# Loading the first two input tiles of a fused attention and gated-linear kernel as half tiles on two DMA queues

## The chip, the cores and the metric

The kernel runs on one core of one Trainium2 chip. The metric is the device time of one execution in microseconds. Each job runs the kernel before and the kernels under test in turn on one chip; different jobs may have different chips. All runs told of here were of the undisturbed (fast) state by the usual test (within 1.5% of the fastest of the same kernel).

Engines: PE does matmuls, PEld loads its weights, DVE, ACT and POOL do element work, SP and ACT issue DMAs. All times inside an execution are counted from the start of its span.

## The reference, cut to what matters

```python
x = A_x                                        # 2048 x 512, bf16
xn = _layernorm(x, axis=-1)
return x + _A_ref(xn, A_wqkv, A_w_phi, A_wo) + _B_ref(xn, B_w_gate, B_w_up, B_w_down)
# _A_ref: linear attention, 32 heads of 16, softmax feature maps; v = xn @ wqkv[:, 1024:1536]
# _B_ref: ((xn @ w_gate) * (xn @ w_up)) @ w_down, inner width 1792
```

Everything needs `xn`, so nothing useful can start before the first rows of `x` have landed, been centred and been transposed.

## The kernel before

The 2048 rows are 16 tiles of 128 rows. For the first four tiles the kernel splits the mean: ACT sums the second 256 columns and DVE the first 256; DVE then centres, PE transposes, ACT or DVE copies the transposed halves out of PSUM, and PE starts on the value projection (`v_matmul`). The scaling by the standard deviation is applied later. The `warm` calls are dummy matmuls.

```python
    sc.pin = True                       # pinned: each engine keeps this order
    load_x(0, 1)                        # tile 0, 128 KB, SP's queue
    load_x(1, 1, ACT)                   # tile 1, 128 KB, ACT's queue
    load_x(2, 1)
    load_v(ACT, 1)                      # value weights, quarters 1, 0, 3, 2
    load_v(SP, 0)
    load_v(ACT, 3)
    load_v(SP, 2)
    load_x(3, 1)
    load_gu(SP, 0, (1,))                # first slice of w_up
    act(sbf("lnv", 0, 1), eps_f, ["eps"], ["pace"])
    load_gu(ACT, 0, (0,))               # first slice of w_gate
    load_gu(SP, 1)
    ...
    def ln_mean_split(t):
        act(xn_tile(t)[:, 256:], x_tile(t)[:, 256:], [("x", t)], [("mu", t)], scale=1.0 / 512.0,
            accum=mu[:, t:t + 1])
        dve(lambda e: e.tensor_scalar(out=xn_tile(t)[:, :256], in0=x_tile(t)[:, :256], scalar1=1.0 / 512.0,
                                      scalar2=0.0, op0=ALU.mult, op1=ALU.add, accum_out=mua[:, t:t + 1]),
            [("x", t)], [("mua", t)], 256)
    ...
    warm(7)                             # 7 dummy matmuls of 512 columns
    warm(1, 512, [("x", 0)])            # one more when tile 0 is there
    sc.pin = True
    ln_mean_split(0)
    ln_mean_split(1)
    ln_center_split(0)                  # DVE; needs both sums
    ln_center_split(1)
    x_transpose(0, 2, 0)                # tile 0, first half; copied out by ACT
    ln_mean_split(2)
    x_transpose(0, 3, 1)
    warm(1, 128)
    x_transpose(1, 4, 0, DVE)           # tile 1, first half; copied out by DVE
    ln_center_whole(2)
    x_transpose(1, 5, 1, DVE)
    warm(1, 128)
    for t in range(2):
        v_matmul(t, t, ((1,), (0,)), stop=False)
    x_transpose(2, 6, 0)
    ...
```

The softmax here doesn't subtract the row's maximum and nothing guards it: scores larger than these inputs give would overflow.

## Time and profile before

| | before |
|---|---|
| time, first job | 214.42 us (214.38 to 214.47, 3 runs) |
| span of the traced execution | 212.6 us |
| PE busy | 98% of the span |
| tiles 0 and 1 landed | 3.68 and 3.84 us |
| first transpose on PE | 4.78 us |
| first gate matmul | 8.98 us |

The page says at once what the limit is. First come the span, PE's line of busy times, and the chain that ended last, by engine:

```profile
span 212.6 us, 4047 instructions
...
PE 208.8 (98%) x1476; PEld 125.6 (59%) x1476; DVE 165.8 (78%) x281; ACT 144.6 (68%) x350; POOL 108.8 (51%) x137
...
PE 97%; DMA 1%; DVE 1%; issue 0%
```

The chain in order of time (start, duration, what) shows, at its start, the only stretch but the last half microsecond (DVE, at 210.0 us) in which that chain is not PE's:

```profile
0.79 2.89 DMA arena<-in_A_x_dram
...
3.70 0.57 DVE arena L427 x3
...
4.46 0.27 DVE arena L434
...
4.78 0.65 PE ps L474 x4
```

Tile 0 lands at 0.79 + 2.89 = 3.68 us, DVE sums tiles 0 and 1 (L427) and centres (L434), PE transposes (L474). The timeline of PE (start, duration, engine, line, operation, shapes, count) goes on from there; the lines of dummy matmuls are left out:

```profile
4.78 0.65 PE L474 MATMUL ps<-arena 128*128 128x128 bf16 x4 [0.39 <-DVE arena L434]
...
5.33 0.63 PE L474 MATMUL ps<-arena 128*128 128x128 bf16 x4
...
5.87 1.33 PE L247 MATMUL ps<-arena 128*128 128x512 bf16 x4
...
7.25 2.33 PE L247 MATMUL ps<-arena 128*128 128x512 bf16 x12
```

The view puts twelve matmuls from 7.25 us on one line. The first eight, of 512 columns, start every 0.216 us; the last four, of 256 columns and from 8.98 us, are the first gate matmuls. The four from 5.87 us are the first value matmuls; they start at 5.87, 6.29, 6.60 and 6.82, so the first ran at half rate (0.427 us for 512 columns) and the full rate was there at about 6.5 us.

### The profile page before, as it was taken

To read this page: it belongs to the slowest core of one execution; us is meant where nothing else is said; L and a number is where in the kernel's file an instruction comes from. 1 tells how busy PE (TensorE), PEld (TensorE's weight loads), DVE (VectorE), ACT (ScalarE), POOL (GpSimd) and SP (SyncE) were. 2 spreads that over 40 slices of the span, in tenths; PEclk is the share of its full clock that TensorE was granted. 3 is DMA by queue.
4 is the path that set the end of the run, shared out by engine and by line. 5 is a ranking of instruction groups with operands and counts; after the bars stand their busy time and mean duration, and the time that the engine had idled before them with its cause. 6 is when DMAs were issued, how large, how long until landed. Compare 5 with 4: busy or idle time off the path is not lost.

```text
span 212.6 us, 4047 instructions
## 1 busy us (share of the span) xinstructions
PE 208.8 (98%) x1476; PEld 125.6 (59%) x1476; DVE 165.8 (78%) x281; ACT 144.6 (68%) x350; POOL 108.8 (51%) x137
## 2 busy tenths in 40 slices
PE   7999999999999999999999999999999999999995
PEld 2665444444554444444444444456888898899884
DVE  3686699998986647758989989896888898897622
ACT  4459998885989999987878977564544444432220
POOL 4030393243312448998895472204658549558540
DMA  5999119479500320331321223414265836556511
GB/s 166 305 283 372 65 35 187 89 200 328 104 3 0 49 49 3 60 59 33 72 53 26 49 52 49 104 54 65 48 80 131 190 70 135 125 128 148 123 49 49
DMA packets 49252, 22.29 MB, mean 105 GB/s; under 512 B 38097, under 2 KB 47697, under 8 KB 49233
## 3 DMA queue, kind: packets, MB, share of 16 engines
q1 hardware_dynamic: 48272, 21.39, 43.4%
q10 hardware_dynamic: 960, 0.66, 1.0%
q8 instruction: 11, 0.18, 0.4%
q14 instruction: 9, 0.07, 0.1%
HBM read 11.03 MB, written 2.10 MB: 62 GB/s over the span
## 4 chain that ended last, share of the span: by engine, by line
PE 97%; DMA 1%; DVE 1%; issue 0%
PE ps L247 91%; PE ps L553 2%; PE ps L611 2%; DMA arena<-in_A_x_dram 1%; PE ps L381 1%; PE ps L474 1%; DVE arena L427 0%; DVE arena L924 0%; DVE arena L434 0%; PE ps L1001 0%
## 5 line engine op out<-in xcount | busy, mean ns | idle before, releaser
L247 PE MATMUL ps<-arena 128*128 128x512 bf16 (+2 forms) x1160 | 200.0, 330 | 0.0
L247 PEld LDWEIGHTS ps<-arena 128*128 128x128 bf16 (+1 forms) x1160 | 110.9, 98 | 73.4 <-ACT arena L228 0.3
L228 ACT ACTIVATE arena<-ps 128x512 bf16<-128x512 f32 (+3 forms) x117 | 59.3, 538 | 17.9 <-PE ps L247 12.4
L228 ACT ACTIVATE arena<-arena 128x32 f32<-128x32 f32 (+8 forms) x131 | 52.4, 424 | 6.0 <-DVE arena L894 3.0
L894 DVE TENSOR_TENSOR arena<-ps,arena 128x512 f16<-128x512 f32 (+1 forms) x56 | 38.3, 685 | 19.5 <-ACT arena L228 14.2
L516 POOL TENSOR_TENSOR arena<-arena 128x1024 bf16<-128x1024 bf16 x16 | 31.0, 1934 | 38.0 <-ACT arena L228 38.0
L228 ACT ACTIVATE arena<-ps,arena 128x512 bf16<-128x512 f32 (+1 forms) x55 | 35.5, 671 | 10.1 <-PE ps L247 10.0
L506 DVE TENSOR_REDUCE arena<-arena 128x64 f32<-128x1024 bf16 x32 | 38.6, 1210 | 3.3 <-ACT arena L228 3.3
L855 POOL TENSOR_TENSOR arena<-arena 128x256 f16<-128x256 f16 x32 | 24.3, 768 | 13.0 <-DMA arena<-arena 11.7
L228 ACT ACTIVATE ps<-ps 128x256 f32<-128x256 f32 x24 | 8.8, 368 | 29.0 <-PE ps L247 29.0
L833 DVE TENSOR_TENSOR arena<-arena 128x896 f16<-128x896 f16 x32 | 23.7, 749 | 3.2 <-PE ps L247 3.1
L924 DVE SCALAR_TENSOR_TENSOR arena<-ps,arena 128x256 bf16<-128x256 f32 (+1 forms) x24 | 13.5, 569 | 10.4 <-PE ps L247 10.0
L773 POOL TENSOR_TENSOR arena<-arena 128x512 f16<-128x512 bf16 x14 | 16.2, 1175 | 4.7 <-DVE arena L894 3.3
L959 POOL TENSOR_TENSOR arena<-arena 128x512 f32<-128x512 f32 x8 | 9.5, 1192 | 17.1 <-ACT arena L228 17.1
L522 POOL TENSOR_TENSOR arena<-arena 128x512 bf16<-128x512 bf16 x16 | 17.2, 1074 | 0.9
L621 DVE TENSOR_TENSOR arena<-ps,arena 128x512 f16<-128x512 f32 x16 | 11.0, 687 | 1.4
L405 DVE BATCH_NORM_STATS2 arena<-arena 128x6 f32<-128x512 bf16 x16 | 10.4, 672 | 0.4 <-DMA arena<-in_A_x_dram 0.4
L520 POOL TENSOR_TENSOR arena<-arena 128x32 f32<-128x32 f32 x16 | 4.2, 266 | 9.5 <-ACT arena L228 9.5
L668 DVE BATCH_NORM_STATS2 arena<-arena 128x6 f32<-128x512 bf16 x14 | 9.0, 681 | 0.0
L553 PEld LDWEIGHTS ps<-arena 128*128 128x128 bf16 x128 | 6.0, 97 | 3.5
L802 DVE TENSOR_TENSOR arena<-arena 128x1792 f16<-128x1792 f16 (+1 forms) x8 | 7.0, 903 | 0.0
L611 PEld LDWEIGHTS ps<-arena 128*128 128x128 bf16 x128 | 6.2, 97 | 1.2
(54 smaller groups left out, 68.1 us busy)
## 6 DMA issues: line engine op xcount, KB each, us to landing
arena<-in_A_x_dram SPq DMA_DIRECT2D x8, 256.0 KB, 3.3
out_dram<-arena SPq DMA_DIRECT2D x15, 128.0 KB, 2.0
arena<-in_B_w_down_dram SPq DMA_DIRECT2D x1, 1792.0 KB, 7.9
arena<-in_A_x_dram SPq DMA_DIRECT2D x3, 512.0 KB, 4.2
arena<-arena SPq DMA_TRANSPOSE x44, 3.0
arena<-in_B_w_gate_dram SPq DMA_DIRECT2D x1, 640.0 KB, 8.7
arena<-in_B_w_up_dram SPq DMA_DIRECT2D x1, 640.0 KB, 9.9
arena<-in_B_w_gate_dram SPq DMA_DIRECT2D x1, 512.0 KB, 5.3
```

The costliest lines, as they stand in the source:

```text
L228: return sc.step(ACT, lambda e: e.activation(out=out_ap, in_=in_ap, func=func, scale=scale, **kw), reads, writes, 130.0 + 0.833 * n)
L247: ins = e.matmul(out_ap, lhsT=l, rhs=r, start=start and i == 0, stop=stop and i == npair - 1, **kw)
L506: dve(lambda e: e.tensor_reduce(out=sm, in_=e_v, axis=AX.X, op=ALU.add), [(name, s, 0), (name, s, 1)], [("sums", sr)], 1024)
L516: pool(lambda e: e.tensor_tensor(out=e_w, in0=e_w, in1=r_w, op=ALU.mult), [(name, s, 0), (name, s, 1), ("rs", n)], [(name, s, 0), (name, s ...
L522: pool(lambda e: e.tensor_tensor(out=e_v[:, :, 1, :], in0=e_v[:, :, 1, :], in1=rat[:, :, None].to_broadcast([128, H, 16]), op=ALU.mult), [ ...
L611: ins = e.matmul(bank(b0 + c // 4, (c % 4) * CW, CW), lhsT=ph[:, c, :], rhs=kvz_v[:, c, :], start=True, stop=True)
L621: dve(lambda e: e.tensor_tensor(out=o_tile(t).rearrange("p (b h f) -> p b h f", b=2, f=16), in0=nd[:, :, :, 0:16], in1=w_v[:, r].unsqueeze ...
L773: pool(lambda e, ft=ft: e.tensor_tensor(out=hH_v[:, ft, 0:512], in0=hT_v[:, ft, 0:512], in1=r2w, op=ALU.mult), [("hT", ft, 0), "r2w", ("x" ...
L833: dve(lambda e, k=k, i0=i0, i1=i1, op=op: e.tensor_tensor(out=s_block(p, k), in0=i0, in1=i1, op=op), ks + more, [s_key(p, k)] + over.get(k ...
L855: pool(lambda e, k=k, i0=i0, i1=i1, op=op: e.tensor_tensor(out=so_block(p, k), in0=i0, in1=i1, op=op), ks + [("so", p, m) for m in more], ...
L894: dve(lambda e: e.tensor_tensor(out=h_v[:, ft, sg * 512:(sg + 1) * 512], in0=bank(bu), in1=g, op=ALU.mult), [("ps", bu), ("g", s)] + ([("j ...
L924: dve(lambda e: e.scalar_tensor_tensor(out=o, in0=src, scalar=inv, in1=resid, op0=ALU.mult, op1=ALU.add), keys + [rkey, "inv"], [("ostg", ...
```

## The change

The intent is to begin sooner: the two halves of a tile go out on two queues at once, and each engine waits only for the half that it sums. The first slice of `w_gate` moves to SP's queue, both tiles use value weight quarter 1 before quarter 0, and a small constant that DVE made while idle is made later.

```diff
+    def load_x_half(t, h, eng):
+        c = slice(h * 256, h * 256 + 256)
+        o, i = x_tile(t)[:, c], rows(x_flat, t, 1)[:, 0, c]
+        sc.dma(eng, lambda e: e.dma_start(o, i), [], [("x", t) if h else ("x", t, 0)], 65536)
 ...
-    load_x(0, 1)
-    load_x(1, 1, ACT)
+    for t in range(2):
+        load_x_half(t, 0, SP)
+        load_x_half(t, 1, ACT)
 ...
+    act(sbf("lnv", 0, 1), eps_f, ["eps"], ["pace"])
+    load_gu(SP, 0, (0,))
     load_gu(SP, 0, (1,))
-    act(sbf("lnv", 0, 1), eps_f, ["eps"], ["pace"])
-    load_gu(ACT, 0, (0,))
 ... (in ln_mean_split, DVE's part)
-            [("x", t)], [("mua", t)], 256)
+            [("x", t, 0) if t < 2 else ("x", t)], [("mua", t)], 256)
 ...
-    for t in range(2):
-        v_matmul(t, t, ((1,), (0,)), stop=False)
+    for q in (1, 0):
+        for t in range(2):
+            v_matmul(t, t, ((q,),), start=q == 1, stop=False)
 ... (the constant epsz: made after the fourth tile's value matmuls, not at the start)
```

More of the change, by code (lines that the diff above doesn't have):

```diff
@@ L361, in _build, with eps_z @@
     pool(select(m4, ALU.is_ge, 0.0, 0, [[-32, 4], [0, HC]], 1), ["const"], ["mask"], CW)
-    dve(lambda e: e.tensor_reduce(out=epsz, in_=m1, axis=AX.XY, op=ALU.add), ["mask16"], ["epsz1"], 64)
-    dve(lambda e: e.tensor_scalar(out=epsz, in0=epsz, scalar1=1e-6, scalar2=None, op0=ALU.mult), ["epsz1"], ["epsz"], 1)
+    def eps_z():
+        dve(lambda e: e.tensor_reduce(out=epsz, in_=m1, axis=AX.XY, op=ALU.add), ["mask16"], ["epsz1"], 64)
+        dve(lambda e: e.tensor_scalar(out=epsz, in0=epsz, scalar1=1e-6, scalar2=None, op0=ALU.mult), ["epsz1"],
+            ["epsz"], 1)
     pool(select(m4, ALU.is_ge, 0.0, 31, [[32, 4], [0, HC]], -1), ["mask"], ["mask"], CW)
@@ L1042, in _build @@
     u1a()
+    eps_z()
     sc.pin = False
```

## The prediction

> **What bounds the kernel now.** The page gives a span of 212.6 us with PE busy 98%; the chain that ended last is PE 97%, DMA 1%, DVE 1%. By the chain in order of time, tile 0's load runs 0.79 to 3.68 us, then DVE sums (0.57 us) and centres (0.27 us), and the first transposes start at 4.78 us. In the PE timeline, from about 6.8 us the 512-column matmuls follow each other every 0.216 us without gaps. So the change can win only in the first 6.8 us, if no load that it delays is then waited for.
>
> **What changes.** By the order of instructions, PE, DVE, ACT and POOL compute as much as before; SP issues two more DMAs, ACT's queue one more half tile and no gate slice. The constant moves from an idle DVE (2.85 to 3.26 us) to about 14 us, costing DVE some 0.2 us off the critical path. PE's order changes only in that both tiles use weight quarter 1 before quarter 0.
>
> **Gain.** Before, tiles 0 and 1 (128 KB each, one per queue) shared the DMA engines and landed at 3.68 and 3.84 us. Now the first 128 KB is all of tile 0. In the packet records a 1024-byte packet takes 46 ns and a 512-byte one (first gate slice) 27 ns: the same bytes cost 17% more, but half a tile is ready sooner. [...] So only order is won. Estimates: tile 0's halves land at 3.3 (SP) and 3.5 us (ACT's first packets come 0.4 us later), tile 1's at 3.8 to 4.0. The in-order DVE sums tile 1 before it centres tile 0, so the first centring waits for tile 1's first half: about 3.8 + 0.34 = 4.12 us against 4.38. First transpose about 4.5 us: 0.25 us earlier.
>
> **What eats it.** PE runs at half rate (0.427 us per 512 columns) until about 6.5 us. [...] if the change of rate stays near 6.5 us, PE enters its dense stretch only 0.13 to 0.2 us earlier. The value weights are issued 0.4 us later but are bandwidth-limited: quarter 1 at 5.04 to about 5.3 us, needed at 5.6; quarter 0 about 5.9, needed at 6.3. First gate slice: 7.4 to about 7.8 us, needed at 8.8. Later loads slip by 0.8 us, with over 2 us of slack on PE.
>
> **Predicted** 214.2 us (before 214.42), 0.1% faster; range 213.9 to 214.55. Faster by over 2%: 0.005; within 2%: 0.99; slower by over 2%: 0.005.
>
> **What would show it.** First DVE sum at 3.3 to 3.4 us, not 3.70; first transpose 4.4 to 4.6, not 4.78; first full-rate matmul still near 6.5; dense stretch and all later pieces of the chain 0.1 to 0.25 us earlier; no PE wait for a weight load.
>
> **What would make it wrong.** Four half loads with as many packets as four whole ones may land no sooner (first DVE sum above 3.6 us, or tile 1's half above 4.1): no gain or a small loss. A late value weight or gate slice would show as a PE wait for a DMA at 5.6 to 9 us. Tiles 4 to 7 landing late could block the in-order DVE near 16 us.

Two passages are cut above, where marked. The forecast's sum is 214.42 us less about 0.2 us at the start of the dense stretch, 214.2 us.

## The result, and the profile after

213.93 us median (213.83 to 214.20, 6 runs) against 214.44 us (213.79 to 214.71, 6 runs) for the kernel before. The ratio is 0.9981 with a 95% interval of 0.9966 to 0.9995. (A ratio here is the mean time of one kernel's fast-state runs over that of the other's in the same rounds, so it is not quite the ratio of the two medians.) So the time falls by 0.2%: clear of zero.

The page after, first its span and PE's busy time, then the chain by engine:

```profile
span 212.2 us, 4050 instructions
...
PE 208.5 (98%) x1476; PEld 125.2 (59%) x1476; DVE 166.0 (78%) x281; ACT 144.7 (68%) x350; POOL 108.7 (51%) x137
...
PE 97%; DMA 1%; DVE 1%; SPq 0%; issue 0%
```

The chain in order of time, after:

```profile
0.79 0.39 SPq L277
...
1.24 2.54 DMA arena<-in_A_x_dram
...
3.81 0.26 DVE arena L436
...
4.23 0.27 DVE arena L443
...
4.55 0.54 PE ps L483 x4
```

The DMA of this chain was issued at 1.24 us: it is tile **1**'s first half (landing at 3.78 us). Tile 0's halves were there at 3.28 and 3.44 us and are no longer on the chain. DVE's timeline after shows why:

```profile
3.30 0.42 DVE L436 TENSOR_SCALAR_CACHE_REDUCE arena<-arena 128x256 bf16<-128x256 bf16 x1 [3.30 <-DMA arena<-in_A_x_dram]
...
3.81 0.42 DVE L436 TENSOR_SCALAR_CACHE_REDUCE arena<-arena 128x256 bf16<-128x256 bf16 x1
...
4.15 1.11 DVE L443 TENSOR_SCALAR arena<-arena 128x256 bf16<-128x256 bf16 x4
5.27 0.42 DVE L436 TENSOR_SCALAR_CACHE_REDUCE arena<-arena 128x256 bf16<-128x256 bf16 x1
...
5.62 0.29 DVE L492 COPY arena<-ps 128x256 bf16<-128x256 bf16 x1
```

Tile 0's sum starts at 3.30 us, but DVE works in program order and waits for tile 1 (3.81) before it centres (4.15). Lower down, the sum of tile 2 (5.27) stands in front of the copy of tile 1's transposed half (5.62). PE's timeline after, without the dummy matmuls:

```profile
4.55 0.54 PE L483 MATMUL ps<-arena 128*128 128x128 bf16 x4 [0.16 <-DVE arena L443]
...
5.06 0.54 PE L483 MATMUL ps<-arena 128*128 128x128 bf16 x4
...
5.56 1.23 PE L247 MATMUL ps<-arena 128*128 128x512 bf16 x4
...
6.84 2.33 PE L247 MATMUL ps<-arena 128*128 128x512 bf16 x12
```

Everything from the twelve matmuls on starts 0.41 us earlier (6.84 against 7.25). The first transpose is 0.23 us earlier, as the prediction had it; the other 0.18 us are made between 4.55 and 6.84 us. There the pieces themselves are shorter: each group of four transposes took 0.54 us instead of 0.65 and 0.63, and the four value matmuls 1.23 instead of 1.33 us although PE waited inside them. PE's full rate was granted at 4.27 us in this trace (its record of the clock), and at about 6.5 us in the one of before. Whether the change did that, or chance, is the question of the experiments.

One more line of each kernel matters: the issue of tile 2 on SP's queue, with its size and the time from issue to landing. Before (issued at 1.24 us), then after (issued at 1.70 us):

```profile
arena<-in_A_x_dram SPq DMA_DIRECT2D x1, 128.0 KB, 3.5
```

```profile
arena<-in_A_x_dram SPq DMA_DIRECT2D x1, 128.0 KB, 3.5
```

The extra half load in front of it cost tile 2 the whole of one issue, 0.46 us: it lands at 5.25 instead of 4.78 us. This did not hold DVE up in this trace: the last of its four centrings runs from 4.92 to 5.26 us, so the sum of tile 2 could not have started before 5.27 us anyway (before the change it started at 5.41 us).

### The profile page after: what moved, and what is told of

Its sections match the earlier page's. It is cut to its first block, busy times and chain, and to the rows that moved or that the text cites. A ratio compares the mean times of both kernels' runs of the same rounds, so it can differ in the third digit from the quotient of the medians.

```text
span 212.2 us, 4050 instructions
## 1 busy us (share of the span) xinstructions
PE 208.5 (98%) x1476; PEld 125.2 (59%) x1476; DVE 166.0 (78%) x281; ACT 144.7 (68%) x350; POOL 108.7 (51%) x137
## 4 chain that ended last, share of the span: by engine, by line
PE 97%; DMA 1%; DVE 1%; SPq 0%; issue 0%
PE ps L247 91%; PE ps L562 2%; PE ps L620 2%; DMA arena<-in_A_x_dram 1%; PE ps L390 1%; PE ps L483 1%; DVE arena L933 0%; SPq L277 0%; DVE arena L436 0%; DVE arena L443 0%; PE ps L1010 0%
```

## The experiments

Twelve kernels ran, three of them unedited. In all of them every output was correct. Where I say "whole" and "half" I mean how tiles 0 and 1 are loaded.

### 1. Both kernels again

No edit. Is the moment of the full rate a property of the kernel or of the execution?

> The kernel before, unchanged, to see in a second trace when PE changes from 0.427 to 0.216 us per 512 columns. In the first trace of before this was near 6.5 us, in the one of after before 4.5 us. Theory phase ([...] it differs from execution to execution of one kernel): [...] not necessarily 6.5; loads land as before (3.68 and 3.84 us within 0.1). Rival theory gap (the change itself brings the moment forward, since PE idles 0.16 us instead of 0.39 us before the first transpose): again 6.5 us within 0.2. Time: ratio 1.000 within 0.15%.

> The changed kernel again. Both theories: first DVE sum 3.30, tile 1's first half 3.78, first transpose 4.55 us, each within 0.1. Theory phase: [...] if it falls late the dense stretch starts up to 0.2 us later than 6.62 us. Rival gap: again before 4.5 us. Time: 0.25 to 0.5 us below before on the same chip.

Cut from theory "phase" here, and from "phase" and "gap" in experiment 3: a mechanism, and the range of moments worked out from it, that no trace had shown. "Phase" is that the moment of the full rate differs between executions of one kernel.

Measured: before again 214.52 us median (213.64 to 214.82, ratio 0.9996); the changed kernel again 213.98 us (213.84 to 214.29, ratio 0.9980, interval 0.9964 to 0.9997). So the gain repeats. But the traced execution of before was one of 213.96 us: full rate at 5.79 us, first gate matmul at 8.60 us. The changed kernel's second trace had full rate at 4.70 us and its first gate matmul at 8.65 us, in 214.00 us. With the full rate early in both, the two kernels start the gate matmuls within 0.05 us of each other, and the changed one is not the earlier.

The theory "gap" (the change itself brings the full rate forward by leaving PE less idle) expected 6.5 us again for before: it was 5.79. The times showed more: those of before are not spread around a middle but fall in two groups. In these two jobs, 7 of 23 executions of before were in the early group (mean 213.88 us) and 16 in the late one (mean 214.58 us); of the changed kernel, 11 of 12 were early (mean 213.96 us). If both kernels had the same odds, so unequal a split would come by chance less than once in a thousand (Fisher's exact test; the border at 214.25 us was chosen after seeing the times; against all 62 executions of before, later jobs included, of which 29 were early, it is about 4 in a thousand). The mean gain of 0.4 us is thus nearly all in how often the late group occurs; inside the early group the changed kernel is 0.09 us *slower* here.

### 2. PE hot before the loads, first attempt

Loads held back by DVE work until about 10 us, PE kept on dummy matmuls meanwhile. The edit, the same in both kernels:

```diff
+    def timer_fn(e):
+        for i in range(7):
+            ins = e.tensor_reduce(out=..., in_=tmr..., axis=AX.X, op=ALU.add)
+        return ins
+    dve(timer_fn, ["timer0"], ["timer"], 1024)
-        sc.dma(eng, ..., [], [("x", t) ...], ...)
+        sc.dma(eng, ..., ["timer"], [("x", t) ...], ...)     # in the loads of x; the rest queue behind
-    warm(7)
+    warm(21)
+    warm(12, 512, ["timer"])
     warm(1, 512, [("x", 0)])
```

> The kernel before with all tile loads (and what is queued behind them) held back by about 9 us of dummy DVE work, while PE runs 33 dummy matmuls, so that PE is at full rate for certain when tile 0 lands. Slower than before by 8 to 10 us, on purpose. Theory phase: the spread of its times shrinks (before: 213.79 to 214.71) since no useful work runs at half rate, to under 0.4 us. First transposes 4 us after the first tile load is issued, as before. It is the reference for a_hot.

> The changed kernel with the same hold. With PE at full rate in both, only loads and order differ. If the gain of the change is 0.23 us from the loads and the rest was the luck of the clock: 0.2 to 0.3 us faster than b_hot by the start of the dense stretch relative to the first load issue. If the full 0.41 us comes from the change by another path than the clock (PE order, late gate slice): 0.4 us or more.

Measured: 223.55 us (222.87 to 224.01, 4 runs) and 223.52 us (223.19 to 224.53, 5 runs). The experiment failed in the traced execution of the first: that PE would "for certain" be at full rate was an assumption, and it was not. Stretches of it, with columns for PE, PEld, DVE, ACT and POOL busy time, then the granted clock, the DMA share and GB/s:

```profile
4.50:11.00 6.50, 3.70 (x18) 1.54 (x17) 5.77 (x7) 0.00 (x0) 0.00 (x0) 1.00 0.00 0
11.20:14.50 3.30, 3.30 (x9) 1.14 (x8) 1.82 (x9) 1.11 (x5) 0.00 (x0) 0.50 0.84 264
14.60:20.00 5.40, 5.37 (x45) 3.40 (x44) 3.06 (x12) 2.71 (x9) 0.00 (x0) 1.00 1.18 294
```

The dummy matmuls ran out at about 7.1 us, PE idled until 10.05 us, and the clock fell to 0.50 from 11.13 to 14.54 us, just where the useful work began. Every execution lists its mean clock: 2 of the first kernel's 4, this traced one among them, and 3 of the second's 5 list 0.992, which is what 3.41 us at 0.50 in a span of 221.8 us comes to; by this estimate these were spoilt alike. The changed kernel's traced execution was not: full rate from 6.42 us to the end, and the first gate matmul at 17.74 us against 18.19 us. The pair cannot be compared.

### 3. Filling or widening PE's idle stretch

Before + one more dummy matmul (the first edit); after − the dummy matmul that waits for tile 0 (the second).

```diff
     warm(1, 512, [("x", 0)])
+    warm(1, 384)
```

```diff
-    warm(1, 512, [("x", 0)])
```

> The kernel before with one more dummy matmul (384 columns, 0.32 us at half rate) behind the one that waits for tile 0, so that PE's idle stretch before the first transpose shrinks from about 0.55 us to about 0.2 us, while every load and every useful instruction stays. So far 23 runs of before fall into two groups (7 at 213.6 to 214.1, 16 at 214.3 to 215.1) and 12 of the changed kernel into one (213.8 to 214.3). Theory gap (the idle stretch decides [...]): the slow group vanishes, median 213.8 to 214.1, ratio near 0.998, rate change before 5.8 us. Theory phase ([...] the two groups are luck): two groups again, median 214.3 to 214.6, ratio 1.000. Theory loads (the change gains by earlier tiles): ratio 1.000.

> The changed kernel without the dummy matmul that waits for tile 0: PE idles about 0.8 us before the first transpose instead of 0.36 us; loads and useful instructions stay, first transpose again at 4.55 us. Theory gap: the slow group appears, most runs at 214.3 to 215, median over 214.3, rate change later than 5.8 us. Theory phase: times as the changed kernel's (213.8 to 214.3). Theory loads: as the changed kernel's, ratio 0.998.

Measured: the filled before 214.59 us (213.75 to 214.73; 2 of 6 early, ratio 0.9993); the changed kernel with the wider gap 213.89 us (213.85 to 214.05; 6 of 6 early, ratio 0.9972, interval 0.9938 to 1.0005). The theory "gap" falls on both sides: filling the gap did not remove the late group, and widening it from 0.36 to 0.79 us did not bring it. The traced execution of the filled kernel (213.75 us) had tile 0 at 3.48 us, full rate at 4.42 us and its first gate matmul at 8.38 us, the earliest of all, with whole tiles.

### 4. The halves alone, and the change without the halves

The halves alone: before with `load_x_half` for tiles 0 and 1 and the split wait of DVE's sum; gate slice, PE's order and the constant as before. The rest alone: the change with whole tiles.

```diff
-    load_x(0, 1)
-    load_x(1, 1, ACT)
+    for t in range(2):
+        load_x_half(t, 0, SP)
+        load_x_half(t, 1, ACT)
```

> The kernel before with the half loads and the split waits alone; the first gate slice stays on the second queue, PE's order and the small constant as before. Theory loads: the halves are the whole gain, ratio 0.998. Theory gap: the earlier tiles shrink PE's idle stretch as in the changed kernel, so the slow group vanishes too, ratio 0.998; but where the rate changes early, the first gate matmul is no earlier than before's 8.60 us. Rival theory order (the gain needs PE's new order, as quarter 0 lands late): ratio 0.999 to 1.000, with PE waiting for the second value weight near 5.9 us.

> The changed kernel with tiles 0 and 1 loaded whole again, one per queue; gate slice on the first queue, PE's new order and the moved constant stay. If the halves are what removes the slow group: two groups as in before, median 214.3 to 214.6, ratio 1.000 within 0.1%, tile 0 landing at 3.5 to 3.7 us. If instead the order of the other loads or of PE does it: one group at 213.8 to 214.2.

Measured: the halves alone 214.03 us (213.86 to 214.27; 5 of 6 early and the sixth only just over the border; ratio 0.9978, interval 0.9947 to 1.0009), in a job in which before was early in 4 of 11. The rest alone 213.84 us (213.75 to 214.49; 5 of 6 early; ratio 0.9972, interval 0.9933 to 1.0011), but in a job in which before itself was early in 7 of 11. So the halves alone went with as few late executions as the whole change, but 5 of 6 against the 6 of 17 early ones of the whole-tile kernels in that job (before and filled) can be chance (about 7 in a hundred). The test of the rest alone is inconclusive, because the odds of before differ from job to job: that the order of the other loads or of PE also does it is not ruled out.

The sixth run of the rest alone (214.49 us) was the traced one, and shows one thing that a late execution can be. Its waits between 8 and 10.5 us (engine, line, awaited: us in total, times, longest):

```profile
PEld ps L247 <- DMA arena<-in_B_w_up_dram: 0.6, 1, 0.6
PE ps L247 <- DMA arena<-in_B_w_up_dram: 0.4, 1, 0.4
```

The first `w_up` slice landed at 9.73 us, where eight of the nine other traces without a hold had it between 8.3 and 8.9 us and the ninth at 9.2. By the packet records nearly all of it had been moved by 7.75 us, and a few last packets followed between 8.75 and 9.5 us. PE stood still for 0.60 us; its first gate matmul (8.51 us) had been early, within 0.13 us of the earliest.

### 5. DVE copies before it sums tile 2

In the changed kernel, DVE's sum of tile 2 is moved behind the copy of tile 1's transposed first half.

```diff
-    ln_mean_split(2)
+    ln_mean_split(2, (ACT,))
     x_transpose(0, 3, 1)
     warm(1, 128)
     x_transpose(1, 4, 0, DVE)
+    ln_mean_split(2, (DVE,))
```

> The changed kernel, with DVE copying tile 1's transposed first half before it sums tile 2 (which lands only at 5.3 us). In the changed kernel that sum holds the copy from about 5.37 to 5.62 us, and PE waits with its second value matmul from 5.77 to 5.96. If that wait is what eats the gain of the earlier tiles: second value matmul at 5.75 to 5.8, dense stretch 0.1 to 0.2 us earlier than in the changed kernel (first gate matmul at 8.4 to 8.5 instead of 8.57 to 8.65 us), times 0.1 to 0.2 us lower. Rival (the first value weight, landing at 5.4 to 5.5, or tile 2's centring binds instead): less than 0.05 us.

Measured: 213.87 us (213.81 to 214.28; 5 of 6 early), against 213.89 us for the variant of experiment 3 in the same job: no difference that six runs can show. The traced execution was the sixth (214.28 us), in which the full rate came late. PE's timeline of it:

```profile
4.57 0.65 PE L491 MATMUL ps<-arena 128*128 128x128 bf16 x4 [0.17 <-DVE arena L451]
...
5.65 1.50 PE L247 MATMUL ps<-arena 128*128 128x512 bf16 x4
...
7.21 2.33 PE L247 MATMUL ps<-arena 128*128 128x512 bf16 x12
```

The copy did come first (5.58 us), but the value matmuls started at 5.65, 6.08, 6.50 and 6.77 us: half rate until about 6.6 us. So the wait that I wanted to remove could not show, and the experiment is inconclusive about it. But the trace is worth having for another reason: with half loads *and* a late full rate, the first gate matmul is at 8.94 us, practically that of before with a late full rate (8.98). In this trace the early tiles did not protect against a late clock.

### 6. PE hot before the loads, second attempt

The hold of experiment 2, with PE busy nearly throughout.

```diff
-    warm(21)
-    warm(12, 512, ["timer"])
-    warm(1, 512, [("x", 0)])
+    warm(40)
+    warm(5, 512, ["timer2"])     # one more piece of DVE work later
+    warm(2, 512, [("x", 0)])
```

> The kernel before with its loads held back to 10.0 us by dummy DVE work, this time with dummy matmuls arranged so that PE is never idle for long (the first such pair lost its full clock again at 11.13 us, which spoilt it). PE is at full rate when tile 0 lands. Over all jobs 34 runs of before fall into a fast group (213.6 to 214.2) and a slow one (214.3 to 214.8, two thirds of the runs). Theory clock (the slow group are runs in which the full clock is granted late, while useful work already runs): one narrow group, spread under 0.3 us. Rival theory landing (in the slow group tile 0 or 1, loaded whole, lands late): two groups again, 0.6 us apart, or a spread over 0.5 us.

> The changed kernel with the same hold. Theory clock: one narrow group, within 0.1 us of b_hot2 (where the clock came early the first gate matmul started at 8.60 and 8.38 us in before and at 8.54 to 8.65 us in the changed kernel and its variants, so the earlier tiles alone win nothing). Rival landing: one narrow group, 0.3 to 0.6 us below b_hot2's median.

Measured: 224.07 us (223.18 to 225.02) and 224.09 us (223.14 to 224.99). No difference shows. The traces have the full rate from 4.69 and 4.72 us on, long before the first load is issued at 10.02 us. PE's timeline of the held-back before, then of the held-back changed kernel:

```profile
13.77 0.54 PE L487 MATMUL ps<-arena 128*128 128x128 bf16 x4 [0.46 <-DVE arena L447]
...
14.72 1.33 PE L248 MATMUL ps<-arena 128*128 128x512 bf16 x4
...
16.11 2.11 PE L248 MATMUL ps<-arena 128*128 128x512 bf16 x10
```

```profile
13.79 0.54 PE L496 MATMUL ps<-arena 128*128 128x128 bf16 x4 [0.48 <-DVE arena L456]
...
14.81 1.22 PE L248 MATMUL ps<-arena 128*128 128x512 bf16 x4
...
16.08 2.11 PE L248 MATMUL ps<-arena 128*128 128x512 bf16 x10
```

Tile 0's first half landed at 12.49 us against 12.66 for the whole tile, and it bought nothing: the first transposes are at 13.77 and 13.79 us, because DVE sums tile 1 first, and tile 1's first half (13.02 us) landed later than tile 1 whole (12.83 us).

But the narrow group that I expected did not come: both kernels have the same three levels, about 0.9 us apart. Both traces, of runs at the middle level, have one PE wait of 0.95 us at 66.9 us, for a DVE multiply (one matmul starts at 66.87 us, the next 1.17 us later instead of 0.22). The weight loader's entry for it, in the waits from 60 to 75 us of the held-back before (in total, times, longest):

```profile
PEld ps L248 <- DVE arena L907: 1.3, 1, 1.3
```

No trace of a kernel without the hold has such a wait. So the hold adds a variation of its own, larger than the gain in question, and the pair shows only that with PE hot the two kernels begin their gate matmuls together (17.84 and 17.81 us) and have the same levels of time. It does not prove that the late group of before is the clock's.

### 7. The kernel before, a third trace

No edit; the last run, in the hope of a trace from the late group.

> The kernel before once more, for a third trace and more times. 45 runs of before so far: 18 in the fast group (213.6 to 214.2), 27 in the slow one (214.3 to 216.4); 12 of the changed kernel: 11 and 1. If this traced run is of the slow group (about 60%), its trace tells where the 0.6 us go. Theory clock: no PE wait behind the first gate matmul, full clock granted after 6.5 us, first gate matmul at 9.0 us or later. Theory landing: a load of the first 9 us (tile 3, the first gate or up slice) lands 0.5 us or more later than in the two other traces, and PE waits for it. Theory later stall: the head as in the fast trace (first gate matmul at 8.6 us), and one PE wait of 0.5 to 1 us later on, as at 66.9 us in the kernels that were held back. If it is of the fast group: first gate matmul at 8.4 to 8.6 us, no stall, and the slow group's cause stays open beyond what the first trace shows.

Measured: 214.04 us median (213.81 to 214.80; 5 of 6 early, ratio 0.9994), and the traced execution was an early one (213.81 us). PE's timeline of it:

```profile
4.61 0.54 PE L474 MATMUL ps<-arena 128*128 128x128 bf16 x4 [0.22 <-DVE arena L434]
...
5.12 0.54 PE L474 MATMUL ps<-arena 128*128 128x128 bf16 x4
...
5.56 1.07 PE L247 MATMUL ps<-arena 128*128 128x512 bf16 x4
...
6.69 2.33 PE L247 MATMUL ps<-arena 128*128 128x512 bf16 x12
```

This is the kernel **before**, and it reaches the twelve matmuls 0.15 us before the changed kernel's trace does (6.69 against 6.84). Its first value matmul starts at 5.56 us, as in the changed kernel, and its four take 1.07 us instead of 1.23.

### All traces without the hold, side by side

| kernel, tiles 0 and 1 | tile 0 (half) landed | first transpose | full rate | first value matmul | first gate matmul | time of this run |
|---|---|---|---|---|---|---|
| before, whole | 3.68 | 4.78 | about 6.5 (*) | 5.87 | 8.98 | 214.34 |
| before again, whole | 3.57 | 4.68 | 5.79 | 5.77 | 8.60 | 213.96 |
| before filled, whole | 3.48 | 4.59 | 4.42 | 5.54 | 8.38 | 213.75 |
| before third, whole | 3.50 | 4.61 | 4.48 | 5.56 | 8.42 | 213.81 |
| rest alone, whole | 3.49 | 4.59 | 4.36 | 5.54 | 8.51 | 214.49 |
| after, halves | 3.28 | 4.55 | 4.27 | 5.56 | 8.57 | 213.90 |
| after again, halves | 3.29 | 4.57 | 4.70 | 5.67 | 8.65 | 214.00 |
| after, wider gap, halves | 3.31 | 4.55 | 5.78 | 5.64 | 8.54 | 213.90 |
| copy first, halves | 3.28 | 4.57 | about 6.6 (*) | 5.65 | 8.94 | 214.28 |
| halves alone | 3.28 | 4.54 | 4.75 | 5.50 | 8.59 | 213.92 |

(*) No clock record in the trace; read from the spacing of the value matmuls.

In every row but one the time is the start of the first gate matmul plus 205.3 to 205.4 us. The exception is the run whose `w_up` slice came late (8.51 + 205.36 + 0.60 = 214.47, measured 214.49). So in these ten traces everything that varies happens before or just after that matmul.

## Why the prediction was right or wrong

The total was inside the range, at its lower end (213.93 of 213.9 to 214.55). The forecast gain was 0.22 us and the measured one 0.4 us of means.

- **The limit: right.** PE is busy 98% of the span before and after, and all but one trace differ only in when PE enters its dense stretch.
- **Landing of the halves: right.** Expected 3.3, 3.5, then 3.8 to 4.0 us; measured 3.28, 3.44, 3.78 and 3.96 us. That "only order is won" by the second queue was my estimate. Tile 1 landed no earlier than before (3.78 us for its first half, 3.66 to 3.84 us for the whole tile in three traces of before), and in the first trace of before the packets of the two queues together already took all the time of the 16 DMA engines (52.9% and 48.0% from 2.50 to 3.68 us, 278 GB/s); but no run here issues the same loads from one queue, so that a second one brings no bandwidth was not shown.
- **First centring and first transpose: right in number, wrong in base.** 4.12 and 4.5 us expected, 4.15 and 4.55 measured. But the base, 4.78 us, was one trace, and the latest of five with whole tiles (4.59 to 4.78 us). Against the other four the halves win 0.02 to 0.14 us at the first transpose.
- **The later loads: half wrong.** "Issued 0.4 us later but bandwidth-limited" expected value weight quarter 1 at about 5.3 us. It landed at 5.42 us, 0.38 us later than before (5.04), so nearly the whole issue delay came through, although the 16 DMA engines were busy for 94% of 2.50 to 5.04 us before and for 89% of 2.50 to 5.42 us after; tile 2's delay was the whole of it (issued 0.46 us and landed 0.47 us later). The first value matmul starts 0.13 to 0.14 us after that weight's landing in both traces of the changed kernel (5.56 after 5.42, 5.67 after 5.53), although ACT's copy had ended at 5.25 us in the first. The wait that I had not foreseen at all is the second value matmul's: the weight loader idles 0.34 us up to 5.96 us for DVE's copy of tile 1 (L492), which stood behind the sum of tile 2. It is the change's own order of PE that asks for this copy so soon: the second value matmul is now tile 1's, where before it was tile 0's second. The late tile 2 is not the cause, for the rest alone (whole tiles, the new order, tile 2 landed at 4.73 us) waits in the same way. Here is the line of the changed kernel's timeline, then that of the rest alone:

```profile
5.96 0.33 PEld L247 LDWEIGHTS ps<-arena 128*128 128x128 bf16 x3 [0.34 <-DVE arena L492]
```

```profile
5.90 0.33 PEld L247 LDWEIGHTS ps<-arena 128*128 128x128 bf16 x3 [0.31 <-DVE arena L491]
```

  With half loads and the old order (the halves alone) the second value matmul came no sooner, at 5.98 us: there it waited for value weight quarter 0, which landed at 5.93 us.

  In the traces with an early full rate these waits give back what the halves won: 8.54 to 8.65 us at the first gate matmul with halves, 8.38 to 8.60 us with whole tiles.
- **The clock: wrong.** "If the change of rate stays near 6.5 us" took a moment of one execution for a property of the kernel. It lay between 4.27 and about 6.6 us in ten traces, with either way of loading. Of the 0.41 us between the first two traces, 0.23 us were before the first transpose (and 0.16 us of that was the late base: 4.78 us against a mean of 4.62 us in the other four traces with whole tiles) and 0.18 us, not foreseen, came with the clock.
- **So the step that failed** is the one from a shift in one trace to a gain in the time. I expected every execution to begin about 0.2 us earlier. That the total still fell inside the range is in part luck: a gain of nearly the forecast size came by another way. What the runs show is a change of odds: early executions are no faster than before's early ones (213.96 against 213.88 us of means in the two jobs that have both kernels), but the late group is nearly absent, 1 of 12 against 16 of 23, at a distance of about 0.7 us. That is 16/23 × 0.70 = 0.49 us, less 0.09 us and less 0.03 us for the changed kernel's one late run (1/12 of about 0.33): 0.37 us. The means of the two jobs differ by 0.38 us.

**What stays open.** Why late executions are rarer with the change, and whether its half loads alone are what does it, is not settled. Two causes of single late executions were seen: a late full rate (214.34 and 214.28 us), and a load whose last packets straggle (214.49 us). But the middle of the late group of before (214.4 to 214.8 us) was never caught in a trace, and the two late full rates that were caught explain 214.3 us rather than 214.6. A still later one would do: my estimate from the two rates (0.427 and 0.216 us) is 0.5 us of time per us of delay, so a full rate at about 7.1 us would give 214.6 us, but no trace shows one after 6.6 us.

On the other hand three late executions of before (214.63, 214.96 and 215.13 us) list a mean clock of 0.999. In the changed kernel's trace the clock falls to 0.50 after the last matmul (at 212.49 us, 0.3 us after the end of the span); if it fell to that in these three, 0.999 says, as my estimate, that the fall came 0.2 to 0.6 us before their end. In all eight traces above that record both steps this fall comes 208.21 us after the full rate, which would put their full rate at 4.0 to 5.0 us (an interval shorter by 3.41 us, the length of the low stretch in experiment 2, would put it at 7.5 to 8.4 us, later than in any trace). By this estimate, which no trace of them confirms, the clock was not late in these three.

"Gap" is ruled out by experiment 3. That the loads simply come earlier is ruled out as a like-for-like gain by the table and by experiment 6. The two-group picture itself rests on 62 executions of before, 29 of them early, with odds that differed by job (1 of 6, 4 of 11, 4 of 11, 7 of 11 and 6 of 11 for the runs of before beside the kernels under test), so a part of the measured gain may belong to the job rather than to the change. Against that, the three half-load kernels of experiments 3 to 5 that shared one job were early in 16 of 18 runs, and the whole-tile kernels of that job, before and filled, in 6 of 17.

No version beat both kernels by more than the runs can show: the copy-first kernel's 213.87 us lies 0.02 us from its neighbour in the same job.

## What to carry to other kernels

When a gain of a few tenths of a microsecond is at stake in the first microseconds of a kernel, one trace of before and one of after are two draws, not a comparison: take several of each, note when PE's full rate was granted in each, and look at the whole list of times, since a lower median can be fewer bad executions rather than a faster good one. Splitting the load brought its first part forward here (landed at 3.28 to 3.31 us against 3.48 to 3.68 us whole), but the extra issue pushed tile 2, which stood behind it on that queue, by one issue (0.46 us), and DVE, which sums the next tile before it centres this one, gave most of the advantage back (first transpose at 4.54 to 4.57 us against 4.59 to 4.78 us). So before splitting, it is worth trying the engine's program in the order in which the pieces will arrive; no run here did that for the sums and centrings of tiles 0 and 1.

## What else the traces show of the clock and the loads

- PE's first dummy matmul started at 0.8 us in all ten traces without the hold; the full rate came 3.4 to about 5.8 us after it, a spread of over 2 us. One kernel (the one before, traced three times) had it at 4.48, 5.79 and about 6.5 us.
- In experiment 2 the clock fell at 11.13 us although PE had been busy again since 10.05 us: of the 3.41 us before the fall PE was idle for about 2.3. In the changed kernel's trace with the same hold PE was idle for about 1.6 of the 3.41 us from 6.42 to 9.83 us, and the clock stayed. What decides between the two was not shown. The steps at 4.30, 11.13 and 14.54 us are 6.83 and 3.41 us apart; in the eight traces without a hold that have both records, full rate and fall are 208.21 us apart.
- One issue took 0.39 to 0.45 us against 2.5 to 3.8 us from issue to landing (tiles 0 to 2 and the first weight quarter), and one more issue in front delayed tile 2's landing by 0.47 us.
- The landing of one and the same load varies from execution to execution. The same whole tile 0 landed 2.69 to 2.89 us after its issue in five traces, the half tile 2.49 to 2.52 us in five, and one 256 KB slice took 6.1 us (the first `w_up` slice in experiment 4) where the same load took 4.8 and 4.5 us in the changed kernel's two traces.
